# A 128-column expert visit in the common form, and two transposes of the next tokens moved into the arms

## The chip, the core and the metric

The kernel runs on one core of a Trainium2 chip, one launch. The metric is device time in microseconds; lower is better.

## What is computed

Attention with rotary embedding over 4 batches, 8 heads, 576 positions, 64 dimensions; then an RMS-normed gated layer on the 2304 tokens; then a layer of eight experts, of which each token takes one:

```python
logits = x @ w_gate + modality_bias[modality_id]
e_idx = np.argmax(logits, axis=1)
...
for e in range(E):
    mask = e_idx == e
    if not mask.any():
        continue
    h = np.maximum(x[mask] @ w1[e], 0.0)
    out[mask] = gate_w[mask, None] * (h @ w2[e])
```

Here x[mask] has 512 columns, w1[e] is 512 by 1024 and w2[e] is 1024 by 512. The change lies in this last loop alone.

## The kernel before

Every float32 product is made of three: an operand is split into a high part (rounded to the matmul's float32 format, on ACT) and a low part (what is left, by a subtraction on DVE), and high by high, low by high and high by low are summed.

The expert layer is a row of **visits** (moe, body). One visit serves up to 384 tokens of one expert; an expert with more tokens gets several. Which expert, and how many tokens, is known only on the chip, so each of the 14 possible visits is written out with five **arms**, one for each size in SIZES (128, 256, 288, 352, 384 tokens), and body's choose branches to one by a value that each engine loads. In the program the 128 arm stands right behind the comparisons; the arms of 384, 352, 288 and 256 follow it in this order, and then the tail, which all arms share. Each engine has its own copy of this program and its own branches. With these inputs visits 0 to 7 run; their sizes are 384, 288, 256, 256, 384, 352, 128 and 352 (visit 0 has no arms).

A common arm (visit) has eight steps of first-layer products: 12 matmuls per step (line 1339), the weights being the stationary operand and the N tokens the moving one, so that the hidden values come out transposed; a ReLU on ACT (line 1342) and a subtraction on DVE (line 1343) then give their high and low parts. Four more steps (two for 256 tokens) make the second-layer sums of the second and third block of 128 tokens: second issues 12 matmuls of 512 columns (line 1426) per step, and put scales the sums on DVE and scatters them by an indirect DMA from POOL. The second layer of the first 128 tokens is made in the tail, for every size.

The 128 arm (small_visit) is different: the tokens are the stationary operand, the weights the moving one, 24 matmuls of 512 columns (line 1378). The hidden values come out with tokens on partitions; after the ReLU (line 1383), eight transposes (turn, line 1368) bring them into the form that second needs.

Around these products each visit prepares the next one:

- gather fetches the next visit's tokens by three indirect DMAs from POOL; xT transposes a block of 128 tokens (4 matmuls against the identity, line 1323, into one of two PSUM banks that take turns, then a copy on ACT and a subtraction on DVE, lines 1325 and 1326). A third xT has to wait until the first one's bank has been read by DVE.
- wsplit splits the next pieces of weights (ACT line 1297, DVE line 1298) into a ring of 11; wload then issues the DMA of a later piece, 512 KB, into the raw buffer that the split has freed. So a load is issued when a split on DVE ends. The table SPLITS says after which step of an arm which pieces are split, by the number of 128-token blocks.

The order on each engine is the order in which this code is written.

Of the kernel before, what the change touches and what calls it, by code (L numbers as in the profile page):

```python
# [16 lines left out]
AF = mybir.ActivationFunctionType  # L17
ALU = mybir.AluOpType
# [5 lines left out]
P = 128  # L24
# [7 lines left out]
def fr(ap):  # L32
    return ap.bitcast(F32)
# [17 lines left out]
class Kernel:  # L51
# [824 lines left out]
NE, VT, NV = 8, 384, 14  # L876
# [4 lines left out]
SPLIT0 = {1: 7, 3: 8, 5: 9, 7: 10, 8: 11, 9: 12, 10: 13, 11: 14, 12: 15, 13: 16}  # L881
SPLITS = [
    {},
    {0: 9, 5: 11, 9: 13},
    {0: 8, 1: 9, 3: 10, 5: 11, 8: 12, 9: 13},
    {0: 8, 1: 9, 3: 10, 5: 11, 8: 12, 10: 13},
]
TURNS = {8: (0,), 9: (1,), 10: (2,)}
SIZES = (128, 256, 288, 352, 384)


# [19 lines left out]
class Fused(Kernel):  # L911
# [443 lines left out]
                yield s  # L1355
                s += 1

    def small_visit(self, v):

        nc, st = self.nc, self.st  # L1360
        xh, xl = self.xTt
        ix, xs = st.pop(("x", v))
        hs = [x[:, 0:512] for x in xs[1:3]]

        def turn(x):
            ps = self.p_h().rearrange("p (k n) -> p k n", k=4)
            for k in range(4):
                nc.tensor.transpose(ps[:, k], hs[x][:, k * P:(k + 1) * P], self.idf)
            h, l = (y[:, :, 0:P] for y in self.hq[x::2])
            nc.scalar.copy(h, ps)  # L1370
            nc.vector.tensor_tensor(l, ps, fr(h), op=ALU.subtract)

        for x in range(2):
            ps = self.p_o()
            for k in range(4):
                wh, wl = (y[:, x * 512:(x + 1) * 512] for y in self.wpc[8 * v + k])
                for i, (l, r) in enumerate(((xh, wh), (xl, wh), (xh, wl))):
                    nc.tensor.matmul(ps, l[:, k, 0:P], r, start=(k == 0 and i == 0), stop=(k == 3 and i == 2))
                if x == 1 and k == 1:
                    turn(0)  # L1380
                if k < 3:
                    yield 4 * x + k
            nc.scalar.activation(hs[x], ps, AF.Relu)
            if x == 1:
                g = self.gates(xs, 1)
            yield 4 * x + 3
        turn(1)
        st["last", v] = ix, g
        yield 8
        yield 9  # L1390

    def tail(self, v):

        ix, g = self.st.pop(("last", v))
        ps = self.p_o()
        more = v + 1 < NV
        if more:
            self.xT(v + 1, 0)
            self.wsplit(8 * v + 14)
            self.xT(v + 1, 1)  # L1400
        self.second(v, ps, 0, 0, P)
        if more:
            self.xT(v + 1, 2)
            self.wsplit(8 * v + 15)
        self.second(v, ps, 1, 0, P)
        self.put(ps, ix, g, 0, P)

    def hidden(self, f):
# [25 lines left out]
    def ahead(self, v, s, nt=3):  # L1434

        if v == 0 and s >= 8:
            for t in TURNS.get(s, ()):
                self.xT(1, t)
        i = SPLITS[nt] if v else SPLIT0
        if s in i:  # L1440
            self.wsplit(8 * v + i[s])
# [16 lines left out]
    def body(self, v):  # L1458

        s = self.state()  # L1460

        def arm(x):
            N = SIZES[x]
            if N == P and v + 1 < NV:
                self.gather(v + 1)
            for y in self.visit(v, N) if N > P else self.small_visit(v):
                if y == 0 and N > P and v + 1 < NV:
                    self.gather(v + 1)
                self.ahead(v, y, (N + P - 1) // P)

        def choose(x):
            if x == 0:
                arm(0)
                return
            with self.tc.If(self.size(v) > x - 1, preferred_fallthrough_block=False) as cmp:  # L1475
                arm(x)
            self.restore(s)
            with cmp.Else():
                choose(x - 1)

        choose(len(SIZES) - 1)
# [166 lines left out]
```

## Time and profile before

| | |
|---|---|
| device time, median of 3 runs | 1110.79 us (1108.62 to 1111.71) |
| the profiled execution's own time | 1116.74 us |
| its span, first to last instruction | 1115.0 us |
| TensorE busy | 1037.2 us, 93% of the span |
| DVE, ACT, POOL busy | 64%, 41%, 30% |
| mean granted clock of TensorE | 0.981 of full speed |
| expert visits 1 to 7 | from about 890 to 1103 us of the span |

The profile's view of time sums instructions by line; a timeline gives them in order, with the idle time of the engine ahead of an instruction and what ended it. "issue" there means that the engine waited for nothing that the profile shows.

### The profile page before, as it was taken

How to read it: one execution, taken by the hardware profiler on the slowest of the kernel's cores; microseconds unless marked ns; L12 is line 12 of the kernel's file. 1: busy time of each engine (PE TensorE's matmuls, PEld its weight loads, DVE VectorE, ACT ScalarE, POOL GpSimd, SP SyncE). 2: the span in 40 equal slices, each digit the busy share in tenths (PEclk: the TensorE clock that was granted, in tenths of full speed). 3: DMA queues.
4: the chain of work that ended last, by engine and by line, in shares of the span. 5: the costliest groups of instructions: out<-in, count | busy, mean ns of one | idle time of the engine just before them, and what ended most of it. 6: DMA issues, size and time to landing. Idle time of an engine off the chain costs nothing. (4 is left out here: it accounts for less than half of the span.)

```text
span 1115.0 us, 18245 instructions
## 1 busy us (share of the span) xinstructions
PE 1037.2 (93%) x6662; PEld 878.8 (79%) x6662; DVE 710.4 (64%) x1362; ACT 459.3 (41%) x959; POOL 331.1 (30%) x372
## 2 busy tenths in 40 slices
PE   4999999989998899999999999999998999998795
PEld 3767777666776689899999999998877787898594
DVE  7686788897765876456465555562457856655652
ACT  2655666555555443322222222222235444444441
POOL 7756567478421401012011111110010222222211
PEclk9899999999999899999999999999999999999988
DMA  5333454444231102111131111100146656655653
GB/s 134 81 99 95 107 134 108 121 121 107 60 103 36 55 29 60 54 38 48 36 129 48 39 38 48 39 20 29 58 157 187 218 179 203 204 179 165 213 182 106
DMA packets 75708, 113.35 MB, mean 102 GB/s; under 512 B 18520, under 2 KB 43376, under 8 KB 75570
## 3 DMA queue, kind: packets, MB, share of 16 engines
q1 hardware_dynamic: 71890, 99.72, 30.2%
q0 software_dynamic: 3680, 11.91, 2.9%
q8 instruction: 72, 1.18, 0.4%
q14 instruction: 66, 0.54, 0.1%
HBM read 85.39 MB, written 12.17 MB: 88 GB/s over the span
## 5 line engine op out<-in xcount | busy, mean ns | idle before, releaser
L771 PE MATMUL gv<-xh,whi 128*128 128x384 f32 x576 | 197.2, 342 | 1.4 <-ACT xh L749 1.4
L771 PE MATMUL gv<-xl,whi 128*128 128x384 f32 x576 | 195.2, 339 | 0.2 <-DVE xl L753 0.2
L771 PE MATMUL gv<-xh,wlo 128*128 128x384 f32 x576 | 194.7, 338 | 0.0
L288 DVE TENSOR_REDUCE m<-s 128x1 fp32r<-128x576 f32 (+1 forms) x160 | 119.9, 752 | 66.4 <-PE s L287 65.1
L670 POOL TENSOR_TENSOR wlo<-cvt,whi 128x256 fp32r<-128x256 f32 x66 | 50.8, 774 | 338.2 <-ACT whi L669 338.1
L781 DVE TENSOR_TENSOR s<-s,gv 128x384 f32<-128x384 f32 x72 | 39.8, 554 | 154.0 <-PE gv L771 145.1
L315 ACT ACTIVATE E<-sT 128x576 f32<-128x576 f32 (+1 forms) x160 | 104.3, 653 | 64.7 <-PE sT L314 60.9
L771 PEld LDWEIGHTS gv<-xh,whi 128*128 128x128 f32 x576 | 108.7, 189 | 6.6 <-issue 3.4
L780 ACT ACTIVATE s<-gv 128x384 f32<-128x384 f32 x72 | 34.9, 492 | 189.4 <-PE gv L771 189.4
L771 PEld LDWEIGHTS gv<-xl,whi 128*128 128x128 f32 x576 | 108.8, 189 | 1.9 <-DVE xl L753 0.4
L771 PEld LDWEIGHTS gv<-xh,wlo 128*128 128x128 f32 x576 | 108.6, 188 | 0.0
L312 PE MATMUL sT<-qkT 128*128 128x288 f32 (+1 forms) x320 | 80.6, 334 | 10.2 <-DVE m L288 6.1
L326 PE MATMUL av<-E,vraw 128*64 128x288 f32 x640 | 88.5, 421 | 1.6 <-ACT sq L337 1.6
L799 PE MATMUL yps<-whi,hh 128*128 128x512 f32 x216 | 87.2, 404 | 2.3 <-ACT yacc L804 1.3
L814 DVE TENSOR_TENSOR yacc<-yacc,yps 128x512 f32<-128x512 f32 x99 | 67.7, 686 | 32.2 <-PE yps L799 30.8
L287 PE MATMUL s<-qkT 128*128 128x288 f32 (+1 forms) x320 | 79.6, 335 | 6.6 <-ACT qkT L273 2.7
L799 PE MATMUL yps<-wlo,hh 128*128 128x512 f32 x216 | 85.3, 395 | 0.0
L799 PE MATMUL yps<-whi,hl 128*128 128x512 f32 x216 | 85.2, 394 | 0.0
L1313 POOL DMA_INDIRECT x<-ysc,ix x27 | 30.3, 1121 | 143.1 <-DVE e L1139 76.7
L314 PE MATMUL sT<-qB,kB 65*128 65x288 f32 (+1 forms) x320 | 70.8, 304 | 1.8 <-issue 1.5
L1432 POOL DMA_INDIRECT out<-cvt,ix x20 | 25.3, 1265 | 156.1 <-DVE cvt L1430 120.2
L326 PEld LDWEIGHTS av<-E,vraw 128*64 128x64 f32 x640 | 43.7, 140 | 34.4 <-issue 6.2
(287 smaller groups left out, 2048.8 us busy)
## 6 DMA issues: line engine op xcount, KB each, us to landing
raw<-in_w SPq DMA_DIRECT2D x52, 512.0 KB
stt<-in_w SPq DMA_DIRECT2D x25, 512.0 KB
stt<-in_w_gate SPq DMA_DIRECT2D x24, 256.0 KB
stt<-in_w_val SPq DMA_DIRECT2D x24, 256.0 KB
stt<-in_w_out SPq DMA_DIRECT2D x24, 256.0 KB
kB<-qkT SPq DMA_DIRECT2D x32, 144.0 KB
qB<-qkT SPq DMA_DIRECT2D x32, 144.0 KB
qkT<-qkT SPq DMA_DIRECT2D x32, 144.0 KB
```

The source lines that it names most:

```text
L287: nc.tensor.matmul(s[:n, u, 0:288], qA[:, j * 128:j * 128 + n], kA[:, u * 288:u * 288 + 288], start=True, stop=True)
L288: nc.vector.tensor_reduce(m[:n, j:j + 1], s[:n, :, 0:288], axis=AX.XY, op=ALU.max)
L312: nc.tensor.matmul(s[:n, u, 0:288], kA[:, j * 128:j * 128 + n], qA[:, u * 288:u * 288 + 288], start=True, stop=False)
L314: nc.tensor.matmul(s[:n, u, 0:288], kB[0:65, j * 128:j * 128 + n], qB[0:65, u * 288:u * 288 + 288], start=False, stop=True)
L315: nc.scalar.activation(e.rearrange("p (u c) -> p u c", u=2), s[:n, :, 0:288], AF.Exp, scale=0.125)
L326: self.nc.tensor.matmul(av[64 * h:64 * h + 64, 0:288], V[:, h, j * 64:j * 64 + 64], E[:, h if j < 4 else 0, j, 288 * u:288 * u + 288], sta ...
L670: nc.gpsimd.tensor_tensor(lo, f, fr(hi), op=ALU.subtract)
L771: nc.tensor.matmul(t[:, :CH], w[:, k], r[:, k], start=(n == 0), stop=(n == 11))
L780: nc.scalar.activation(s, ps[0][:, :CH], AF.Silu)
L781: nc.vector.tensor_tensor(s, s, ps[1][:, :CH], op=ALU.mult)
L799: nc.tensor.matmul(ps, l, r[:, 2], start=(n == 0), stop=(n == tot - 1))
L814: nc.vector.tensor_tensor(old[:, t], old[:, t], ps, op=ALU.add)
```

## The change

small_visit is removed: the 128 arm is visit(v, 128), eight steps of 12 matmuls with 128 moving columns. Two of the three xT of the next tokens, blocks 0 and 1, move from the tail into the arm, by the table TURNS: for 128 tokens both after step 7, for 256 after steps 8 and 9, for larger sizes after steps 10 and 11. The third, block 2, stands first in the tail, and the 24 second-layer matmuls follow it without another transpose between them. The splits of the 128 arm stand after steps 0, 5 and 7 (before: 0, 5 and 9). gather in the 128 arm stands after the first step.

```diff
--- before.py
+++ after.py
@@ -881,11 +881,11 @@
 SPLIT0 = {1: 7, 3: 8, 5: 9, 7: 10, 8: 11, 9: 12, 10: 13, 11: 14, 12: 15, 13: 16}
 SPLITS = [
     {},
-    {0: 9, 5: 11, 9: 13},
+    {0: 9, 5: 11, 7: 13},
     {0: 8, 1: 9, 3: 10, 5: 11, 8: 12, 9: 13},
     {0: 8, 1: 9, 3: 10, 5: 11, 8: 12, 10: 13},
 ]
-TURNS = {8: (0,), 9: (1,), 10: (2,)}
+TURNS = [{8: (0,), 9: (1,), 10: (2,)}, {7: (0, 1)}, {8: (0,), 9: (1,)}, {10: (0,), 11: (1,)}]
 SIZES = (128, 256, 288, 352, 384)
 
 
@@ -1355,54 +1355,17 @@
                 yield s
                 s += 1
 
-    def small_visit(self, v):
-
-        nc, st = self.nc, self.st
-        xh, xl = self.xTt
-        ix, xs = st.pop(("x", v))
-        hs = [x[:, 0:512] for x in xs[1:3]]
-
-        def turn(x):
-            ps = self.p_h().rearrange("p (k n) -> p k n", k=4)
-            for k in range(4):
-                nc.tensor.transpose(ps[:, k], hs[x][:, k * P:(k + 1) * P], self.idf)
-            h, l = (y[:, :, 0:P] for y in self.hq[x::2])
-            nc.scalar.copy(h, ps)
-            nc.vector.tensor_tensor(l, ps, fr(h), op=ALU.subtract)
-
+    def tail(self, v):
+
+        ix, g = self.st.pop(("last", v))
+        if v + 1 < NV:
+            self.xT(v + 1, 2)
+            self.wsplit(8 * v + 14)
+        ps = self.p_o()
         for x in range(2):
-            ps = self.p_o()
-            for k in range(4):
-                wh, wl = (y[:, x * 512:(x + 1) * 512] for y in self.wpc[8 * v + k])
-                for i, (l, r) in enumerate(((xh, wh), (xl, wh), (xh, wl))):
-                    nc.tensor.matmul(ps, l[:, k, 0:P], r, start=(k == 0 and i == 0), stop=(k == 3 and i == 2))
-                if x == 1 and k == 1:
-                    turn(0)
-                if k < 3:
-                    yield 4 * x + k
-            nc.scalar.activation(hs[x], ps, AF.Relu)
-            if x == 1:
-                g = self.gates(xs, 1)
-            yield 4 * x + 3
-        turn(1)
-        st["last", v] = ix, g
-        yield 8
-        yield 9
-
-    def tail(self, v):
-
-        ix, g = self.st.pop(("last", v))
-        ps = self.p_o()
-        more = v + 1 < NV
-        if more:
-            self.xT(v + 1, 0)
-            self.wsplit(8 * v + 14)
-            self.xT(v + 1, 1)
-        self.second(v, ps, 0, 0, P)
-        if more:
-            self.xT(v + 1, 2)
-            self.wsplit(8 * v + 15)
-        self.second(v, ps, 1, 0, P)
+            self.second(v, ps, x, 0, P)
+            if x == 0 and v + 1 < NV:
+                self.wsplit(8 * v + 15)
         self.put(ps, ix, g, 0, P)
 
     def hidden(self, f):
@@ -1434,7 +1397,7 @@
     def ahead(self, v, s, nt=3):
 
         if v == 0 and s >= 8:
-            for t in TURNS.get(s, ()):
+            for t in TURNS[0].get(s, ()):
                 self.xT(1, t)
         i = SPLITS[nt] if v else SPLIT0
         if s in i:
@@ -1461,12 +1424,14 @@
 
         def arm(x):
             N = SIZES[x]
-            if N == P and v + 1 < NV:
-                self.gather(v + 1)
-            for y in self.visit(v, N) if N > P else self.small_visit(v):
-                if y == 0 and N > P and v + 1 < NV:
+            nt = (N + P - 1) // P
+            for y in self.visit(v, N):
+                if y == 0 and v + 1 < NV:
                     self.gather(v + 1)
-                self.ahead(v, y, (N + P - 1) // P)
+                self.ahead(v, y, nt)
+                if v + 1 < NV:
+                    for t in TURNS[nt].get(y, ()):
+                        self.xT(v + 1, t)
 
         def choose(x):
             if x == 0:
```

On TensorE, the whole 128 arm of visit 1 stood like this (po, ph, pt and pc are PSUM banks, W and Wl weight pieces, idf the identity, hq and xT the transposed hidden values and tokens, x gathered tokens):

```order
L1378 MATMUL po_8761<-Wl_8743,xT 128x512 x3
L1378 MATMUL po_8761<-Wl_8744,xT 128x512 x3
L1378 MATMUL po_8761<-Wl_8745,xT 128x512 x3
L1378 MATMUL po_8761<-W_8426,xT 128x512 x3
L1378 MATMUL po_8759<-Wl_8743,xT 128x512 x3
L1378 MATMUL po_8759<-Wl_8744,xT 128x512 x3
L1368 MATMUL ph_8758<-idf,x_8751 128x128 x4
L1378 MATMUL po_8759<-Wl_8745,xT 128x512 x3
L1378 MATMUL po_8759<-W_8426,xT 128x512 x3
L1368 MATMUL ph_8756<-idf,x_8752 128x128 x4
L1475 UNCONDITIONAL_BRANCH
```

Now it ends like this, after seven steps of the same four rows:

```order
L1339 MATMUL ph_8756<-xT,Wl_8743 128x128 x3
L1339 MATMUL ph_8756<-xT,Wl_8744 128x128 x3
L1339 MATMUL ph_8756<-xT,Wl_8745 128x128 x3
L1339 MATMUL ph_8756<-xT,W_8426 128x128 x3
L1323 MATMUL pc_6112<-idf,x_8439 128x128 x4
L1323 MATMUL pt_6111<-idf,x_8440 128x128 x4
L1440 UNCONDITIONAL_BRANCH
```

The 24 products and 8 transposes of before are 96 products, and eight transposes of the next tokens stand ahead of the branch.

On TensorE, the end of the 384 arm and the tail of visit 1 stood like this:

```order
L1426 MATMUL po_8759<-W_8429,hq 128x512 x6
...
L1426 MATMUL po_8759<-W_8430,hq 128x512
L1475 UNCONDITIONAL_BRANCH
...
L1323 MATMUL pc_6112<-idf,x_8439 128x128 x4
L1323 MATMUL pt_6111<-idf,x_8440 128x128 x4
L1426 MATMUL po_8760<-W_8427,hq 128x512 x6
L1426 MATMUL po_8760<-W_8428,hq 128x512 x6
L1323 MATMUL pc_6112<-idf,x_8441 128x128 x4
...
L1426 MATMUL po_8760<-W_8430,hq 128x512
L1265 TENSOR_LOAD vi
L1475 COMPARE_AND_BRANCH x4
```

And now:

```order
L1389 MATMUL po_8759<-W_8428,hq 128x512 x6
L1323 MATMUL pc_6112<-idf,x_8439 128x128 x4
L1389 MATMUL po_8759<-W_8429,hq 128x512 x6
...
L1389 MATMUL po_8759<-W_8430,hq 128x512
L1323 MATMUL pt_6111<-idf,x_8440 128x128 x4
L1440 UNCONDITIONAL_BRANCH
...
L1323 MATMUL pc_6112<-idf,x_8441 128x128 x4
L1389 MATMUL po_8761<-W_8427,hq 128x512 x6
L1389 MATMUL po_8761<-W_8428,hq 128x512 x6
L1389 MATMUL po_8761<-W_8429,hq 128x512 x6
...
L1389 MATMUL po_8761<-W_8430,hq 128x512
L1265 TENSOR_LOAD vi
L1440 COMPARE_AND_BRANCH x4
```

The second step of the last block stands between two transposes, and the branch follows the second of them; the tail has one transpose and then 24 products in a row up to the next visit's TENSOR_LOAD and comparisons.

On DVE, the end of the 128 arm, from step 5 on, is now (g is the gate, raw and stt are raw weights):

```order
L1298 TENSOR_TENSOR Wl_8741<-stt,Wl_8741 128x1024
L1298 TENSOR_TENSOR Wl_8742<-raw_8422,Wl_8742 128x1024
L1343 SCALAR_TENSOR_TENSOR hq<-ph_8758,hq 128x128
L1343 SCALAR_TENSOR_TENSOR hq<-ph_8756,hq 128x128
L1298 TENSOR_TENSOR Wl_8743<-raw_8423,Wl_8743 128x1024
L1298 TENSOR_TENSOR Wl_8744<-raw_8424,Wl_8744 128x1024
L1326 TENSOR_TENSOR xT<-pc_6112,xT 128x4x128
L1326 TENSOR_TENSOR xT<-pt_6111,xT 128x4x128
L1440 UNCONDITIONAL_BRANCH
```

The two subtractions of xT stand behind four splits.

## Rows read from the trace of the kernel before

**Rows 1.** Timeline of TensorE, the visits: start us, us, engine, line, what, [idle <-released by].

```profile
923.29 11.64 PE L1339 MATMUL ph<-xT,Wl 128*128 128x256 f32 x96 [2.35 <-issue]
934.77 2.96 PE L1426 MATMUL po<-Wl,hq 128*128 128x512 f32 x12
...
949.69 1.31 PE L1339 MATMUL ph<-xT,W 128*128 128x256 f32 x9 [2.33 <-issue]
...
998.94 2.98 PE L1426 MATMUL po<-Wl,hq 128*128 128x512 f32 x12
1001.75 0.60 PE L1323 MATMUL pt<-idf,x 128*128 128x128 f32 x4
1002.19 0.60 PE L1323 MATMUL pc<-idf,x 128*128 128x128 f32 x4
...
1005.75 3.06 PE L1426 MATMUL po<-Wl,hq 128*128 128x512 f32 x12
1011.76 15.63 PE L1339 MATMUL ph<-xT,Wl 128*128 128x352 f32 x96 [2.95 <-issue]
...
1045.36 0.84 PE L1378 MATMUL po<-W,xT 128*128 128x512 f32 x3
...
1053.26 0.66 PE L1368 MATMUL ph<-idf,x 128*128 128x128 f32 x4 [1.71 <-ACT x L1383]
1059.77 1.08 PE L1323 MATMUL pt<-idf,x 128*128 128x128 f32 x4 [5.85 <-issue]
...
1061.36 4.63 PE L1426 MATMUL po<-Wl,hq 128*128 128x512 f32 x12
...
1069.05 15.63 PE L1339 MATMUL ph<-xT,W 128*128 128x352 f32 x96
```

**Rows 2.** Branches of line 1475 on TensorE's queue, five stretches: ns min/median/max.

```profile
L1475 PEldq COMPARE_BRANCH  x2: 64/2613/5162, 917.8 to 918.0; - x2
...
L1475 PEldq COMPARE_BRANCH  x1: 3553/3553/3553, 997.6 to 997.6; - x1
...
L1475 PEldq COMPARE_BRANCH  x1: 6189/6189/6189, 1005.5 to 1005.5; - x1
...
L1475 PEldq COMPARE_BRANCH  x1: 6333/6333/6333, 1053.3 to 1053.3; - x1
...
L1475 PEldq COMPARE_BRANCH  x1: 433/433/433, 1066.0 to 1066.0; - x1
```

**Rows 3.** DMA, 997.5 to 999.2 us: queue, packets, MB, share of the engines.

```profile
q8 instruction: 1, 0.02, 3.5%
```

**Rows 4.** DMA, 999.2 to 1003 us.

```profile
q1 hardware_dynamic: 144, 0.52, 53.8%
```

**Rows 5.** DMA, 1006 to 1009.3 us.

```profile
q1 hardware_dynamic: 143, 0.52, 64.5%
```

**Rows 6.** DMA, 1009.3 to 1010.4 us.

```profile
q8 instruction: 1, 0.02, 5.4%
```

**Rows 7.** Groups by line and form: busy us, mean ns | idle before.

```profile
L1426 PEld LDWEIGHTS po<-W,hq 128*128 128x128 f32 x180 | 33.2, 188 | 6.7
...
L1298 DVE TENSOR_TENSOR Wl<-raw,Wl 128x1024 fp32r<-128x1024 f32 x24 | 29.3, 1222 | 5.5 <-ACT Wl L1297 5.4
...
L1297 ACT CAST Wl<-raw 128x1024 fp32r<-128x1024 f32 x24 | 24.9, 1043 | 0.0
...
L1343 DVE SCALAR_TENSOR_TENSOR hq<-ph,hq 128x384 fp32r<-128x384 f32 x16 | 8.8, 552 | 6.2 <-ACT hq L1342 4.6 <-issue 1.6
...
L1326 DVE TENSOR_TENSOR xT<-pc,xT 128x512 fp32r<-128x512 f32 x11 | 7.6, 689 | 4.4 <-ACT xT L1325 4.4
...
L1343 DVE SCALAR_TENSOR_TENSOR hq<-ph,hq 128x256 fp32r<-128x256 f32 x16 | 6.6, 421 | 8.3 <-ACT hq L1342 8.3
...
L1426 PEld LDWEIGHTS po<-W,hq 128*32 128x32 f32 x24 | 2.6, 109 | 2.9
```

**Rows 8.** Window 1054 to 1060 us: busy us of each engine, granted clock, DMA.

```profile
1054.00:1060.00 6.00, 0.23 (x1) 0.26 (x2) 3.44 (x6) 2.47 (x3) 0.00 (x0) 0.55 0.99 353
```

More of the change, by code (lines that the diff above doesn't have):

```diff
@@ L1356, in visit @@
                 s += 1
-    def small_visit(self, v):
-        nc, st = self.nc, self.st
-        xh, xl = self.xTt
-        ix, xs = st.pop(("x", v))
-        hs = [x[:, 0:512] for x in xs[1:3]]
-        def turn(x):
-            ps = self.p_h().rearrange("p (k n) -> p k n", k=4)
-            for k in range(4):
-                nc.tensor.transpose(ps[:, k], hs[x][:, k * P:(k + 1) * P], self.idf)
-            h, l = (y[:, :, 0:P] for y in self.hq[x::2])
-            nc.scalar.copy(h, ps)
-            nc.vector.tensor_tensor(l, ps, fr(h), op=ALU.subtract)
-        for x in range(2):
-            ps = self.p_o()
-            for k in range(4):
-                wh, wl = (y[:, x * 512:(x + 1) * 512] for y in self.wpc[8 * v + k])
-                for i, (l, r) in enumerate(((xh, wh), (xl, wh), (xh, wl))):
-                    nc.tensor.matmul(ps, l[:, k, 0:P], r, start=(k == 0 and i == 0), stop=(k == 3 and i == 2))
-                if x == 1 and k == 1:
-                    turn(0)
-                if k < 3:
-                    yield 4 * x + k
-            nc.scalar.activation(hs[x], ps, AF.Relu)
-            if x == 1:
-                g = self.gates(xs, 1)
-            yield 4 * x + 3
-        turn(1)
-        st["last", v] = ix, g
-        yield 8
-        yield 9
     def tail(self, v):
         ix, g = self.st.pop(("last", v))
+        if v + 1 < NV:
+            self.xT(v + 1, 2)
+            self.wsplit(8 * v + 14)
         ps = self.p_o()
-        more = v + 1 < NV
-        if more:
-            self.xT(v + 1, 0)
-            self.wsplit(8 * v + 14)
-            self.xT(v + 1, 1)
-        self.second(v, ps, 0, 0, P)
-        if more:
-            self.xT(v + 1, 2)
-            self.wsplit(8 * v + 15)
-        self.second(v, ps, 1, 0, P)
+        for x in range(2):
+            self.second(v, ps, x, 0, P)
+            if x == 0 and v + 1 < NV:
+                self.wsplit(8 * v + 15)
         self.put(ps, ix, g, 0, P)
```

## The prediction, made before the changed kernel ran

> **What bounds the kernel now.** I read four views: the timeline of TensorE over the expert visits, TensorE's branches, the DMA queues around two of them, and the groups by form. In the timeline TensorE works without a break inside a visit; the gaps the change can touch stand at the ends of arms and tails, and nearly all say "issue": ahead of visit 2 (2.35 us), visit 3 (2.33) and visit 5 (2.95), and 1.71 and 5.85 in the 128 arm, which is visit 6 [rows 1]. That visit takes 1069.05 - 1045.36 = 23.7 us up to the next one's first product.
>
> The gaps are branches. TensorE's queue runs ahead of the engine: the branch that ends visit 4's arm began at 997.6 [rows 2], while the arm's last matmul ended about 1001.75, 4.15 us later. Twelve 512-column matmuls take 1001.75 - 998.94 = 2.81 us, 0.234 each [rows 1], so some 17.7 matmuls were queued. A far jump has to bring a page of instructions (one packet of 0.02 MB [rows 3]): that branch took 3.55 us, the one into visit 5's arm 6.19, the one out of the 128 arm 6.33 [rows 2]. The page comes by DMA and waits behind a weight load that is already moving. For visit 4's arm it moved before 999.2 and the load after that [rows 3, 4]: short. For visit 5's entry the load moved first, and the page only after 1009.3 [rows 5, 6]; the branch ended at 1011.7, 2.3 us after the load: long. So a branch costs what its duration exceeds the work queued behind it, and its duration depends on whether it or a load comes first.
>
> The last gap has a second price. Between 1054 and 1060 the granted clock was 0.55 [rows 8], that is mostly the lower level (1.2 GHz), after TensorE had done 0.23 us of work. The work from 1059.77 to 1069.05, 9.3 us, is three transposes of blocks (0.44 each, by 1002.19 - 1001.75) and 24 matmuls (5.6), 6.9 us at full clock [rows 1]: 2.4 us lost.
>
> **The change, part by part.**
>
> *Entries of visits 2, 3 and 5.* Before, the last 17.7 queued matmuls of a tail were 12 products and 5.7 transposes (0.11 each): 3.4 us. Now all are products: 4.15, less some 0.8 us for the value's load and the comparisons. More important, the load. Before, the tail's first split freed a raw buffer about when the branch came: branch at 1005.5, load moving from 1006 on [rows 2, 5]. Now that split stands behind the third xT: on DVE it follows put and two xT of 0.69, and takes 1.22 [rows 7], while the branch comes 0.7 earlier, so I put the load's issue about 1 us after the branch. The page then goes first, a fetch is 3.55 us, and 0.2 us stays exposed. Visit 2 gains 2.35 - 0.2 = 2.15, visit 5 gains 2.95 - 0.2 = 2.75. Visit 3 follows a 256 arm, which splits once more after its last step; that load is still in front of the page, and I give this entry 1.0. Sum: -5.9. Bounds: -0.7 each by cover alone (-2.1), and all three gaps gone (-7.6).
>
> *Ends of the arms of visits 4, 5 and 7.* Now the last 17.7 are 4 transposes, 12 products and 1.7 transposes: 0.44 + 2.81 + 0.2 = 3.45 us, and the branch comes at 1002.6 - 3.45 = 999.1 in visit 4's times (the arm's work ends 0.88 later, by two xT). The load there is issued by a split behind the put of the second block, which the change doesn't move; it was moving from 999.2 on [rows 4], and a page comes about a microsecond after its branch. So the page that was ahead of the load is now behind it: to 1003 [rows 4], and 2.3 us more as at visit 5's entry: 1005.3. TensorE is done at 1002.6, a gap of 2.7. For visits 5 and 7 I take 2.0 each, their loads being no later but perhaps shorter. Sum: +6.7. Bounds: 3.55 against 3.45 of cover, 0.1 each (+0.3); 3.0 each (+9.0). Visit 1 (288) jumps only over the 256 arm, and the 256 arms fall into the tail: no far jump, nothing.
>
> *Visit 6, the 128 arm.* Removed: 24 products and 8 transposes with a wait for ACT between (1.71). Added: 96 products of 128 columns, each with its own weight load. No row shows such a pair. From above: 256 columns take (934.77 - 923.29)/96 = 0.120. From below: 0.234 at 512 and 0.120 at 256 give 0.00045 per column, so 0.062 at 128 if columns alone counted. Weight loads take 188 ns for 128 columns and 109 for 32 [rows 7], 0.82 ns per column, 105 ns for 128; between the bounds I take the load, with the few ns between pairs 0.112: 10.8 us, and 0.88 for two xT. A page of the Trainium skill ("TensorE: Matmul & The Clock Gate", section on the back-to-back issue gap) gives some 81 ns per pair at 128 columns in a sustained stream; by that the products would take 7.8 us and visit 6 end about 2.3 earlier. No run here shows it.
>
> What follows decides more. The tail's xT of block 2 needs the PSUM bank of block 0, and block 0's DVE subtraction stands behind four splits. Step 5 ends at 6 x 12 x 0.112 = 8.1; ACT's ReLU, gate and first split (1.04) take it to about 10.1; then DVE has four splits of 1.22, two hidden subtractions (552 at 384 and 421 at 256 columns give 0.29 at 128) and one xT of 0.69 [rows 7]: 6.2, so 16.3. TensorE has finished at 11.7: a gap of 4.6 in place of 1.71 and 5.85. The arm's branch (9.7 to at most 16) is hidden in it. Then 0.44 + 24 x 0.234 = 6.1: 22.4. A gap of this size I expect to cost the clock again, 2.4: 24.8 against 23.7, +1.1. Bounds: -3.5 (pairs of 81 ns or less, and no fall) to +3.
>
> *Visit 7's entry.* The same jump took 6.19 in visit 5 and 0.433 here [rows 2]. It passes the 128 and the 384 arm: 32 + 144 matmuls before, 104 + 152 now, each with a weight load, so some 350 and 510 instructions. I count it as far now: 3.55 us against 3.4 of cover, 0.1 (bounds 0 and 2.8, the long fetch). The Trainium skill ("Runtime: NRT & Kernel Launch", instruction fetch mechanics) says instructions come in blocks of 256, two at a time, and that a taken branch outside the two stalls for a fetch. By it this jump is always far and the longer arms speak against the change; the two durations here agree with it. The sum is the same by both, since the cover is counted from rows.
>
> Splits, ReLUs, gather and scatters keep their number; they lie beside TensorE's work outside visit 6, and if that cover went, the next late thing would be the first xT of the next visit.
>
> **Sum:** -5.9 + 6.7 + 1.1 + 0.1 = +2.0 us. The profiled execution's own time, 1116.74 (span 1115.0 and 1.7 around it), would become 1118.7. The median of the runs is 1110.79, six below it; I carry the difference over: **1112.8**.
>
> **Rivals.**
>
> *The arm-end branches stay ahead of the loads.* The race is lost by under a microsecond (999.1 plus about 1, against 999.2); a longer queue wins it. Then +0.3 instead of +6.7: -4.4, 1106.4. For it: the pages came first in the rows of before [rows 3, 4]. Against: one transposed block moved ahead of the branch is already 0.44.
>
> *Pages wait at both ends (slower).* The tail's load comes before the entry's branch as it did at visit 5 [rows 5, 6]; the entries then keep only the better cover, -2.1, beside +6.7 and +1.1: +5.8, 1116.6. It decides if the tail's split ends more than about 1 us earlier than I worked out.
>
> *Half clock after the new gaps.* The clock fell in the gap of 5.85 [rows 8], and no such loss stands behind that of 2.95: visit 5's 96 matmuls of 352 columns took 15.63 us, as visit 7's did [rows 1]. If gaps of 2 to 2.7 suffice, three times 2.4 more: +9.2, 1120.0.
>
> That the change doesn't do what it says: the 128 arm runs once with these inputs, at 1045.36 [rows 1], so it acts, but in one visit only.
>
> **Numbers.** A measurement here tells about 0.3%, 3.3 us, from no change. Forecast 0.48, first rival 0.25, second 0.18, third 0.09. The forecast's own range, 1109.5 to 1115.5, leaves a little on the slower side. Faster by over 0.3%: the first rival, nearly all, 0.22; slower: the other two and a little, 0.29; the same 0.49. The range goes from the first rival's centre, 1106, to a little over the second's, 1118.5.
>
> **What would show it.** Gaps ahead of visits 2 and 5 under 1 us and ahead of 3 about 1.3; new gaps of about 2 to 2.7 between the second transposed block of an arm and the third in visits 4, 5 and 7; in visit 6 products of 0.112 each and a gap of about 4.6 ahead of the tail's transposes, ended by DVE's xT, with a fall of the clock. A pair price over 0.12 in the 128 arm, gaps at all entries as before, or no gaps at the arms' ends, would prove it wrong.

## The result, and the profile after

The changed kernel takes 1126.82 us (median of 6 runs, 1123.03 to 1130.47), the kernel before in the same runs 1111.76 (1108.62 to 1114.94): the ratio is 1.0132, 95% interval 1.0103 to 1.0161. It is slower by 15 us. The forecast was 1112.8, the range ended at 1118.5.

The profiled execution after took 1128.17 us (span 1126.3, mean granted clock 0.979). The profiled execution of before stood 5 us over its median, this one 1.4, so I don't compare the spans but the visits. From visit 1's first product to visit 7's, 178.96 us before (890.09 to 1069.05) became 190.44 (887.61 to 1078.05): 11.5 us more. Visit 7 itself, from its first product to the last, took 33.7 us and takes 37.9.

The timeline of TensorE after, in the columns of [rows 1]; line 1389 is what line 1426 was (second-layer products), 1323 a transposed block, 1339 a first-layer product:

```profile
887.61 2.53 PE L1339 MATMUL ph<-xT,Wl 128*128 128x288 f32 x9 [1.98 <-issue]
...
914.41 0.66 PE L1323 MATMUL pc<-idf,x 128*128 128x128 f32 x4 [0.40 <-DVE cvt L1393]
914.83 5.71 PE L1389 MATMUL po<-W,hq 128*128 128x512 f32 x24
921.09 11.63 PE L1339 MATMUL ph<-xT,Wl 128*128 128x256 f32 x96 [0.55 <-issue]
...
940.69 0.66 PE L1323 MATMUL pt<-idf,x 128*128 128x128 f32 x4 [1.54 <-DVE Wl L1298]
...
947.65 1.30 PE L1339 MATMUL ph<-xT,W 128*128 128x256 f32 x9 [0.74 <-issue]
...
951.13 0.39 PE L1339 MATMUL ph<-xT,W 128*128 128x256 f32 x1 [0.87 <-issue]
...
968.47 0.66 PE L1323 MATMUL pc<-idf,x 128*128 128x128 f32 x4 [1.54 <-DVE W L1298]
...
1006.21 0.63 PE L1323 MATMUL pt<-idf,x 128*128 128x128 f32 x4 [2.57 <-issue]
1006.59 4.59 PE L1389 MATMUL po<-W,hq 128*128 128x512 f32 x12
...
1013.81 15.53 PE L1339 MATMUL ph<-xT,Wl 128*128 128x352 f32 x96
...
1044.03 0.63 PE L1323 MATMUL pc<-idf,x 128*128 128x128 f32 x4 [2.79 <-issue]
1044.41 7.33 PE L1389 MATMUL po<-W,hq 128*128 128x512 f32 x24
1051.58 0.44 PE L1339 MATMUL ph<-xT,W 128*128 128x128 f32 x3
...
1063.54 0.66 PE L1323 MATMUL pc<-idf,x 128*128 128x128 f32 x4 [0.26 <-DMA x<-ysc,ix]
1068.62 1.08 PE L1323 MATMUL pt<-idf,x 128*128 128x128 f32 x4 [4.42 <-DVE xT L1326]
...
1074.78 1.56 PE L1389 MATMUL po<-W,hq 128*128 128x512 f32 x6
1078.05 4.11 PE L1339 MATMUL ph<-xT,W 128*128 128x352 f32 x24 [1.72 <-issue]
...
1108.15 0.63 PE L1323 MATMUL pc<-idf,x 128*128 128x128 f32 x4 [2.41 <-issue]
1108.53 7.40 PE L1389 MATMUL po<-Wl,hq 128*128 128x512 f32 x24
```

Read against [rows 1]:

- The entries of visits 2, 3 and 5 waited 2.35, 2.33 and 2.95 us and now wait 0.55, 0.74 and 0 (the row of 1013.81 has no bracket): -6.3.
- New gaps stand between the second and the third transposed block of visits 4, 5 and 7: 2.57 + 2.79 + 2.41 = +7.8.
- Behind each of them 24 second-layer products take 7.2 to 7.4 us where, at 914.83, 24 take 5.71: +1.5, +1.6 and +1.7, in all +4.8.
- New waits ended by DVE stand ahead of the third block where the arm doesn't jump (visits 1, 2 and 3): 0.40 + 1.54 + 1.54 = +3.5.
- In visit 3's arm a stall of 0.87 is new, and visit 7's entry waits 1.72 where it waited not at all: +2.6.
- Visit 6 up to that wait takes 1078.05 - 1.72 - 1051.58 = 24.75 against 23.69: +1.1.
- The half clock in visit 1's arm: 9 products of 2.53 us where before they took 1.47 (row below): +1.1 in these alone.

That is 14.6 in sum, of the 15.7 by which visits 1 to 7 differ in these two profiles and of the 15 between the medians. The same nine products in the timeline of the kernel before:

```profile
890.09 1.47 PE L1339 MATMUL ph<-xT,Wl 128*128 128x288 f32 x9 [0.86 <-issue]
```

The branches that end the arms of visits 4, 5, 6 and 7, and the one into visit 7's arm, as rows of line 1440 on TensorE's queue, ns as min/median/max (before: 3553 for visit 4's, 433 for visit 7's entry [rows 2]):

```profile
L1440 PEldq COMPARE_BRANCH  x1: 5985/5985/5985, 1000.1 to 1000.1; - x1
...
L1440 PEldq COMPARE_BRANCH  x1: 5768/5768/5768, 1037.7 to 1037.7; - x1
...
L1440 PEldq COMPARE_BRANCH  x1: 4900/4900/4900, 1063.5 to 1063.5; - x1
...
L1440 PEldq COMPARE_BRANCH  x1: 5807/5807/5807, 1102.2 to 1102.2; - x1
...
L1440 PEldq COMPARE_BRANCH  x2: 67/2181/4295, 1073.6 to 1073.7; - x2
```

DMA after in 1000 to 1003.1 us, and then in 1003.1 to 1004.7: first the weight load (q1), then the page of instructions (q8). Before, the page came first [rows 3, 4]:

```profile
q1 hardware_dynamic: 144, 0.52, 78.9%
...
q8 instruction: 1, 0.02, 3.7%
```

And the granted clock in visit 1's arm, behind the new gaps and behind visit 6's (window; busy us of PE, PEld, DVE, ACT, POOL; clock; DMA share; GB/s), half of full, that is 1.2 GHz; before, only visit 6 had such a stretch [rows 8]:

```profile
887.60:891.00 3.40, 3.39 (x14) 3.39 (x15) 0.00 (x0) 0.11 (x1) 0.80 (x1) 0.50 0.76 177
...
1007.00:1010.40 3.40, 3.40 (x10) 2.61 (x9) 2.61 (x3) 2.39 (x3) 0.00 (x0) 0.50 0.17 63
1044.60:1048.00 3.40, 3.40 (x10) 2.66 (x9) 2.39 (x3) 2.48 (x3) 0.00 (x0) 0.50 0.02 4
1068.50:1071.90 3.40, 3.28 (x10) 2.83 (x11) 1.25 (x2) 2.12 (x3) 0.00 (x0) 0.50 0.59 202
1109.50:1112.80 3.30, 3.30 (x9) 2.55 (x9) 3.03 (x3) 1.83 (x2) 0.00 (x0) 0.50 0.06 19
```

### The profile page after: what moved, and what is told of

It is laid out like the page before. It is cut to its first block, busy times and chain, and to the rows that moved or that the text cites. A ratio compares the mean times of both kernels' runs of the same rounds, so it can differ in the third digit from the quotient of the medians.

```text
span 1126.3 us, 18410 instructions
## 1 busy us (share of the span) xinstructions
PE 1047.0 (93%) x6726; PEld 890.2 (79%) x6726; DVE 709.9 (63%) x1368; ACT 459.7 (41%) x963; POOL 331.7 (29%) x372
## 5 line engine op out<-in xcount | busy, mean ns | idle before, releaser
L326 PE MATMUL av<-E,vraw 128*64 128x288 f32 x640 | 86.2, 413 | 0.2 <-ACT sq L337 0.2
L1339 PE MATMUL ph<-xT,W 128*128 128x384 f32 (+4 forms) x384 | 66.6, 319 | 4.3 <-issue 3.3
```

The costliest lines, as they stand in the source:

```text
L326: self.nc.tensor.matmul(av[64 * h:64 * h + 64, 0:288], V[:, h, j * 64:j * 64 + 64], E[:, h if j < 4 else 0, j, 288 * u:288 * u + 288], sta ...
L1339: nc.tensor.matmul(ps[:, :N], w, x[:, k, 0:N], start=(i == 0), stop=(i == 11))
```

## The experiments

Two theories were to be told apart. Theory 1: the moved transposes cost the time, in two ways; (a) the arm-end branch comes later than a weight load, so its page waits, a gap opens and the clock falls behind it; (b) the third block needs the PSUM bank of the first, which DVE has not yet read. Theory 2: the 128-column form costs it, with 96 weight loads in place of 24 and longer code to jump over. Ratios are to the kernel before, run on the same chip in the same rounds, with 95% intervals; the expectations in microseconds were written beside its 1111.8, while on the two chips of these runs it took 1114 to 1115, so the ratios decide.

### The new 128 arm alone

The kernel before, with `visit(v, 128)` in place of `small_visit` and its tail unchanged:

```diff
-    {0: 9, 5: 11, 9: 13},
+    {0: 9, 5: 11, 7: 13},
...
-            for y in self.visit(v, N) if N > P else self.small_visit(v):
-                if y == 0 and N > P and v + 1 < NV:
+            for y in self.visit(v, N):
+                if y == 0 and v + 1 < NV:
```

> The new 128 arm alone: it runs the common form (96 products of 128 columns), the three transposes of the next tokens stay in the tail. Theory 1 (the moved transposes are the cost): arms and tails of the other visits keep the queue of before, so no gaps of 2.4 to 2.8 us at the arm ends of visits 4, 5 and 7, no half clock behind them, entries of visits 2, 3 and 5 wait 2 to 3 us as before; visit 6 takes 22 to 26 us; median 1109 to 1115 beside 1111.8 of the kernel before. Theory 2 (the 128-column form is the cost, with 96 weight loads in place of 24 and the longer jump): most of the 15 us is there already, 1121 to 1128.

Measured: 1.0012 (0.9998 to 1.0027), 1.3 us, which can't be told from nothing. Visit 6 took 24.2 us up to visit 7's first product (1051.83 to 1076.05), 23.7 before, with 1.49 at visit 7's entry. Theory 2 falls as the main cause. The profiled execution also showed something that the kernel before had not. Its timeline at visits 2 and 7, and the granted clock behind the entries of visits 2, 3 and 5:

```profile
925.39 13.04 PE L1339 MATMUL ph<-xT,Wl 128*128 128x256 f32 x96 [1.97 <-issue]
...
1076.05 15.63 PE L1339 MATMUL ph<-xT,W 128*128 128x352 f32 x96 [1.49 <-issue]
```

```profile
925.40:930.00 4.60, 4.60 (x26) 4.60 (x27) 1.17 (x4) 1.32 (x2) 0.99 (x1) 0.63 0.45 162
953.40:957.00 3.60, 3.60 (x18) 3.60 (x19) 0.24 (x1) 0.73 (x2) 0.00 (x0) 0.53 0.51 181
1016.90:1022.00 5.10, 5.10 (x23) 5.10 (x24) 1.58 (x4) 1.40 (x2) 0.98 (x1) 0.67 0.24 91
```

Behind gaps of 1.97, 2.16 and 2.57 us the clock fell; behind the same three gaps before, which were longer, it did not (11.64 us for visit 2's 96 products [rows 1], 13.04 here). This execution took 1123.24 us, the longest of the twelve, whose median is 1115.98; so three half clocks at once need not be this kernel's usual case.

### The moved transposes alone

The changed kernel, with `small_visit` and its splits back for 128 tokens; its other arms and the tail stay as they are:

```diff
-    {0: 9, 5: 11, 7: 13},
+    {0: 9, 5: 11, 9: 13},
...
-TURNS = [{8: (0,), 9: (1,), 10: (2,)}, {7: (0, 1)}, {8: (0,), 9: (1,)}, {10: (0,), 11: (1,)}]
+TURNS = [{8: (0,), 9: (1,), 10: (2,)}, {8: (0,), 9: (1,)}, {8: (0,), 9: (1,)}, {10: (0,), 11: (1,)}]
...
-            for y in self.visit(v, N):
+            for y in self.visit(v, N) if N > P else self.small_visit(v):
```

> The moved transposes alone: two transposed blocks of the next tokens stand in every arm and one first in the tail, but the 128 arm keeps its own form with 512 columns. Theory 1: gaps of 2.4 to 2.8 us at the arm ends of visits 4, 5 and 7, each with some 3.4 us of half clock behind it, waits of about 1.5 us for a PSUM bank ahead of the third transposed block after the 256 arms; median 1120 to 1127. Theory 2: only the entries' gain remains, 1104 to 1111. Either way visit 7's entry tells whether the longer 128 arm is what makes that jump far: 4 us of branch as in the changed kernel, or 0.4 as before, worth about 1.7 us.

Measured: 1.0092 (1.0070 to 1.0113), 10 us. The timeline has the gaps of theory 1 at the same places, with the half clock behind them (12 products in 4.59 us), here visit 4's arm end:

```profile
1000.08 0.63 PE L1323 MATMUL pt<-idf,x 128*128 128x128 f32 x4 [2.62 <-issue]
1000.46 4.59 PE L1423 MATMUL po<-W,hq 128*128 128x512 f32 x12
```

Two parts of the expectation failed. The waits ahead of the third block were 0 after the 288 arm and 0.41 after the 256 arms, not 0.40 and 1.54, though these arms are the changed kernel's own; what that means is said under the third block's bank below. And visit 7's branch took 4.72 us though the 128 arm had its old form: with eight more transposes in each arm that jump is far, and with the new form alone it is far too (4.61). Its length alone doesn't decide: the same jump over 176 matmuls was far at visit 5's entry of the kernel before (6.19) and near at visit 7's (0.43) [rows 2]. What put it within reach there was not looked into.

The two parts alone give 10 and 1.3 us, together 11.6 of 15. What they cost only together is mostly these waits (0.40 + 1.13 + 1.13 more in the changed kernel) and visit 7's entry (1.72 against 0.52).

### The load behind the arm-end branch

The changed kernel, with an arm's last split one step later; the split sets off the weight load:

```diff
-    {0: 8, 1: 9, 3: 10, 5: 11, 8: 12, 10: 13},
+    {0: 8, 1: 9, 3: 10, 5: 11, 8: 12, 11: 13},
```

> The changed kernel, with the last split of the arms of 288 to 384 tokens one step later, after step 11 in place of step 10: the weight load that it sets off comes later than the arm-end branch. Theory 1a (the page of instructions waits behind the weight load): the branches at the arm ends of visits 4, 5 and 7 go from 5.8 us to 3.4 to 4, their gaps from 2.4 to 2.8 us to under 0.6, and the half clock behind them goes: 7 to 12 us less than the changed kernel, 1115 to 1120. Rival (the branch is long by itself, because of the queue it stands in): branches stay at 5.8 us, median 1125 to 1129. A third outcome, the load only moves on to the next jump: arm-end gaps gone but entries of visits 5 and 6 wait 2 us more, 1119 to 1124.

Measured: 1.0065 (1.0045 to 1.0084); against 1.0132 that is 7.4 us less. The branches of visits 4, 5 and 7 took 3.91, 3.59 and 3.34 us, the page came at once, with no row of q1 in the window (DMA, 1002.4 to 1005 us, the row of q8), and no half clock stood in visits 1 to 5 or 7. Branch, DMA and timeline at visit 4's arm end:

```profile
L1440 PEldq COMPARE_BRANCH  x1: 3913/3913/3913, 1002.4 to 1002.4; - x1
```

```profile
q8 instruction: 1, 0.02, 2.3%
```

```profile
1007.54 0.66 PE L1323 MATMUL pt<-idf,x 128*128 128x128 f32 x4 [1.54 <-DVE W L1298]
```

Theory 1a is shown: one step of a split, with no instruction added or taken away, makes the branch 2.1 us shorter. In the gap's place stands a wait of 1.54 for the bank. The moved split makes most of it: visit 1's arm, which has no far branch at its end, now waits 1.53 there where it waited 0.40 (the next experiment shows how). So an arm end gives back about 1.0 of its gap and 1.6 of clock, three times 2.6, beside the 7.4 measured; smaller changes elsewhere, this one and visit 7's entry (0.76 in place of 1.72) among them, nearly cancel.

### The third block in a bank of its own

```diff
-            self.xT(v + 1, 2)
+            self.xT(v + 1, 2, self.p_h)
```

> The changed kernel, with the third transposed block written to a PSUM bank of the other ring, so that it need not wait for DVE to read the first block. Theory 1b (the waits of 1.54, 1.54 and 0.40 us ended by DVE ahead of the third block are that bank): these three waits go, 3 us or more; in visit 6 the wait of 4.42 us ends at the branch at the earliest (1063.55 + 4.90 = 1068.45 against 1068.62), so it stays but says issue; median 1122 to 1124. Rival (the wait is DVE's for another reason, or the branches end no earlier): 1126 to 1128.

Measured: 1.0105 (1.0084 to 1.0125), 3.0 us less than the changed kernel; the intervals overlap, so the time alone shows little, and the timeline decides. The three waits went (at visit 1's end the third block follows the second at once), and one gap grew: visit 3's entry, 0.74 in the changed kernel, behind a branch of 5.62 us:

```profile
910.90 0.60 PE L1323 MATMUL ph<-idf,x 128*128 128x128 f32 x4
...
943.72 1.30 PE L1339 MATMUL ph<-xT,W 128*128 128x256 f32 x9 [2.26 <-issue]
```

In visit 6 the wait stayed, 4.58, and the row now says issue: it is the branch's.

So the shared bank causes the three waits, but not in the way of theory 1b: DVE was not late in reading it. In the changed kernel the subtraction that reads visit 2's first block (in bank pt) was over at 937.34. TensorE's third block, in the same bank, began at 940.69, just behind a split that stands later on DVE:

```profile
936.65 0.69 DVE L1326 TENSOR_TENSOR xT<-pt,xT 128x512 fp32r<-128x512 f32 x1 [1.25 <-ACT xT L1325]
...
939.42 1.22 DVE L1298 TENSOR_TENSOR Wl<-stt,Wl 128x1024 fp32r<-128x1024 f32 x1
```

The tail is one program for all five arms. In the changed kernel each of the three waits ended with the last but one DVE instruction of the arm (put's scaling after the 288 arm, a split after the 256 arms), and in the 128 arm the last but one is the subtraction of block 0. With the old 128 arm, where two splits stand between the two subtractions, the waits ended with the last but two or were gone. So it looks as if the tail waits for one count of DVE's instructions that is safe after every arm, and the 128 arm, though visits 1 to 3 don't run it, sets the count. For this speaks that the edits of the second experiment lie in the 128 arm alone and shortened the waits of visits 1, 2 and 3, and that the split moved later, which became the last but one after the larger arms, lengthened visit 1's. No run moved block 0 in the 128 arm by itself.

### Both

```diff
-    {0: 8, 1: 9, 3: 10, 5: 11, 8: 12, 10: 13},
+    {0: 8, 1: 9, 3: 10, 5: 11, 8: 12, 11: 13},
...
-            self.xT(v + 1, 2)
+            self.xT(v + 1, 2, self.p_h)
```

> The changed kernel with both edits: the arm's last split after step 11, the third transposed block in a PSUM bank of the other ring. Theory 1: with the split moved six waits of 1.53 us for the bank were left (visits 1 to 5 and 7), so 6 x 1.53 = 9.2 us go on top of the 7.4 that the split's place gave: 16.6 of the changed kernel's 15 us excess, that is no more than 2 to 3 us from the kernel before on either side, ratio 0.997 to 1.002. Rival (behind each bank wait stands a branch that the wait only hides, so one gap takes the other's place): the two edits do not add up, 5 to 8 us over the kernel before, ratio 1.004 to 1.007.

Measured: 1.0034 (1.0014 to 1.0053), just outside what theory 1 expected and short of the rival, with an interval that reaches into both. The six waits of 1.53 went (0.34, 0.76 and 0.39 were left at the three arm ends), but only 3.5 us came off (1.0065 to 1.0034), not 9.2. The timeline and the branch at visit 5's entry say why:

```profile
1007.86 17.19 PE L1339 MATMUL ph<-xT,Wl 128*128 128x352 f32 x96 [1.80 <-issue]
```

```profile
L1440 PEldq COMPARE_BRANCH  x1: 5469/5469/5469, 1002.3 to 1002.3; - x1
```

The load that the late split sets off is now under way when the tail's branch comes, since the tail begins 1.5 us earlier; that page waits in its place (loads from 1001.99 on, the page at 1005.42), and the clock fell once more (17.19 us where 15.63 stood [rows 1]). Visit 3's entry waited 2.07.

### Both, with the old 128 arm

The same with `small_visit`, as in the second experiment:

```diff
-            for y in self.visit(v, N):
+            for y in self.visit(v, N) if N > P else self.small_visit(v):
```

> Both edits, and the 128 arm in its own form with 512 columns. Theory 1 with the 128-column form at no profit: visit 6 is 1.5 to 2 us shorter than with both edits and the new form (24.7 against 26.5 us in the runs so far), 3 to 0 us under the kernel before, ratio 0.996 to 1.000. Rival (visit 6 costs the same by either form once the bank is free): as with the new form, within 1 us of it.

Measured: 1.0053 (1.0033 to 1.0072), which neither expected. Visit 6 was 1.1 us shorter than with the new form (25.1 against 26.2), but in this profile the clock fell there for 10.2 us, and visit 7's second half lost 1.8 more. The two intervals overlap: what the old form is worth in this arrangement stays open.

### The load ahead of both branches

The changed kernel, its third block in the other bank, and the last two splits of an arm earlier, ahead of the scaling of the second block on DVE:

```diff
-    {0: 8, 1: 9, 3: 10, 5: 11, 8: 12, 9: 13},
-    {0: 8, 1: 9, 3: 10, 5: 11, 8: 12, 10: 13},
+    {0: 8, 1: 9, 3: 10, 5: 11, 7: 12, 8: 13},
+    {0: 8, 1: 9, 3: 10, 5: 11, 7: 12, 8: 13},
...
-            self.xT(v + 1, 2)
+            self.xT(v + 1, 2, self.p_h)
```

> The changed kernel with the third block in the other bank, and the last two splits of an arm one to two steps earlier (after steps 7 and 8, ahead of the scaling of the second block) instead of later. Theory 1: the last load of the arm is then over before the arm-end branch begins, and the next one, set off in the tail, is issued after the entry's branch, so no jump meets a moving load: branches of 3.3 to 4.2 us at the arm ends of visits 4, 5 and 7 and at the entries of visits 2, 3 and 5, gaps there under 0.8 us. With both edits before (split later) 1.80 and 2.07 us stood at two entries and 3.4 us of half clock behind one; so 3 to 5 us less than that, ratio 0.997 to 1.001 to the kernel before. Rival (the jumps are long whenever two visits' loads are near): ratio 1.002 to 1.005 as with the split later.

Measured: 0.9993 (0.9970 to 1.0017), 15 us under the changed kernel. Branches at visit 4's arm end and visit 5's entry, then the timeline at that entry (0.24 at the arm end):

```profile
L1440 PEldq COMPARE_BRANCH  x1: 3657/3657/3657, 993.4 to 993.4; - x1
...
L1440 PEldq COMPARE_BRANCH  x1: 3687/3687/3687, 999.9 to 999.9; - x1
```

```profile
1003.69 1.55 PE L1339 MATMUL ph<-xT,Wl 128*128 128x352 f32 x8 [0.23 <-issue]
```

At the six jumps that the expectation names the branches took 3.33 to 3.69 us, and with the bank free as well the whole excess is gone. What keeps this version from a gain is visit 6 with visit 7's entry, 27.9 us (1037.66 to 1065.51) against 23.7: its gap ahead of the third block was 4.56, behind a branch of 5.04, and visit 7's entry waited 1.34 behind one of 5.63. And in visit 3's arm TensorE stood for 1.62 a few products after its entry, as it did for 0.87 in the changed kernel.

### The tail's order alone

The kernel before with its arms unchanged; in the tail the three blocks first, the third in the other bank:

```diff
             self.xT(v + 1, 0)
-            self.wsplit(8 * v + 14)
             self.xT(v + 1, 1)
+            self.xT(v + 1, 2, self.p_h)
+            self.wsplit(8 * v + 14)
         self.second(v, ps, 0, 0, P)
         if more:
-            self.xT(v + 1, 2)
             self.wsplit(8 * v + 15)
```

> The kernel before, with its arms as they are; only its tail is reordered: the three transposed blocks first, the third in a bank of the other ring, then the two splits and the 24 second-layer products without a transpose between. Theory 1: the arm ends keep their queue (no gaps there, no half clock), and the entries of visits 2, 3 and 5 get the longer queue and the page ahead of the load: gaps of 2.35, 2.33 and 2.95 us become 0.3 to 1.2 each, 4 to 6 us less than the kernel before, ratio 0.994 to 0.997; visit 6 keeps its gap of about 5.85. Rival (three transposes in a row wait for ACT and DVE as they did in the changed kernel, or the load still goes first): entries as before, ratio 0.999 to 1.003.

Measured: 0.9927 (0.9902 to 0.9953), 8 us faster than the kernel before, a little more than theory 1 expected. The timeline of the three entries and of visit 6:

```profile
922.47 11.63 PE L1339 MATMUL ph<-xT,Wl 128*128 128x256 f32 x96 [0.64 <-issue]
...
948.05 1.31 PE L1339 MATMUL ph<-xT,W 128*128 128x256 f32 x9 [1.53 <-issue]
...
1007.54 15.63 PE L1339 MATMUL ph<-xT,Wl 128*128 128x352 f32 x96 [0.39 <-issue]
...
1054.02 1.12 PE L1323 MATMUL pc<-idf,x 128*128 128x128 f32 x4 [4.66 <-issue]
```

The entries give 7.63 - 2.56 = 5.1 us, visit 6's gap 1.2 (5.85 before). So most of what the change had to give at the entries (6.3) comes from the tail's order; the transposes need not leave the tail for it, and left there they don't take the cover from the arm-end branch. Two things moved in that order: no transpose stands among the 24 products, and the splits, which set off the loads, stand behind the third block. The branches into visits 2, 3 and 5 became shorter, 3.83, 4.89 and 4.10 us for 5.16, 5.17 and 6.19; that is 3.7 of the 5.1, so the smaller part is cover. That the loads' place shortened them agrees with the experiments above; no run here separates the two.

### That tail with the new 128 arm, and with earlier splits

To the last kernel the edit of the first experiment is added:

> The reordered tail with the new 128 arm. By the runs so far the form alone cost 1.3 us (ratio 1.0012, 0.9998 to 1.0027), of which 1.49 us was visit 7's entry, where the branch became far; the reordered tail should hide most of that. Theory 1: within 1 us of the reordered tail with the old 128 arm, 3 to 6 us under the kernel before, ratio 0.994 to 0.998. Rival (three transposes in front of a visit 6 with short cover wait longer): 2 us or more above it.

Measured: 0.9927 (0.9901 to 0.9953), the same; visit 7's far jump (3.74 us) is hidden, as expected. Then, in the arms of 256 tokens, the last two splits earlier:

```diff
-    {0: 8, 1: 9, 3: 10, 5: 11, 8: 12, 9: 13},
+    {0: 8, 1: 9, 3: 10, 5: 11, 7: 12, 8: 13},
```

> The reordered tail with the new 128 arm, and in the arms of 256 tokens the last two splits after steps 7 and 8 in place of 8 and 9. Theory 1: the entry of visit 3, which waited 1.58 us behind a branch of 4.87 us, meets no moving load any more: 0.3 to 0.7 us; all else as in the kernel with the reordered tail and the new arm, so 1 us less than it, ratio 0.990 to 0.995 to the kernel before. Rival (that branch is long for another reason): 1.4 to 1.7 us as it was.

Measured: 0.9911 (0.9881 to 0.9942). Visit 3's entry and its branch:

```profile
943.67 1.30 PE L1339 MATMUL ph<-xT,W 128*128 128x256 f32 x9 [0.38 <-issue]
```

```profile
L1439 PEldq COMPARE_BRANCH  x1: 3487/3487/3487, 940.0 to 940.0; - x1
```

The entry went as expected, 1.58 to 0.38, but visit 7's entry waited 1.03 in place of 0.22 in this profile; the 1 us in time is within the intervals. These three are faster than both kernels.

## Why the prediction was wrong

**Entries of visits 2, 3 and 5: right.** Forecast -5.9, measured -6.3. Visits 2 and 5 keep 0.55 and 0, where 0.2 each was worked out; visit 3 gained 1.6 where 1.0 was given.

**Arm ends of visits 4, 5 and 7: right as far as the gap goes.** Forecast 2.7 + 2.0 + 2.0, measured 2.57 + 2.79 + 2.41 (7.8 for 6.7), with the load ahead of the page and a branch of 5.99 us, from 1000.05, where 6.2 was worked out. The split moved alone shows the cause.

**Visit 6: the time right, by luck in part.** It took 24.75 us for a forecast of 24.8. The products came at 1.34 us per 12 (the first 12 at 1.29), that is 0.112 each, as worked out. The Trainium skill ("TensorE: Matmul & The Clock Gate", back-to-back issue gap) has 81 ns per pair at 128 columns; the trace does not agree for these float32 products, and the measurement decides. The gap was 4.42 for 4.6, but it came another way. DVE's subtraction of block 0 ended at 1066.62 + 0.68 = 1067.30, 15.7 us after the visit's start where 16.3 was worked out, and alone would have made a gap of 3.1 (row: 1063.54 + 0.66 = 1064.20). What ended last was the arm's branch, which the prediction had as hidden: it began at 1063.55, with the second block, which had waited for its gathered tokens ([0.26 <-DMA]), took 4.90 and ended at 1068.45. The row of 1068.62 names DVE's xT, but with a bank of its own the third block waited 4.58, for "issue". The clock fell as expected, at 1.6 us rather than 2.4.

**The step that failed most: the half clock.** It was kept out of the sum and given a chance of 0.09, on the ground that no such loss stood behind visit 5's gap of 2.95. It came behind all three new gaps, at 1.5 to 1.7 us each (4.8), and once in visit 1's arm (1.1); the rival had 2.4 each. The evidence was one place in one execution. The new 128 arm alone shows how weak that was: the same three entries, with shorter gaps, had a half clock behind each of them. In the twelve traces 19 gaps of 1.8 to 3.2 us stand at the entries and arm ends of visits 2 to 5 and 7, and 13 have a half clock behind them. So in these kernels such a gap has to be priced with its clock as a likely case, not as a remote one. The 4.8 is read from one execution; but over the six runs of each kernel the mean granted clock was 0.978 and 0.977 where the three arm-end gaps stood (moved transposes alone, third block's own bank) and 0.984 in the same rounds with the split moved, where they didn't. The changed kernel's own six runs, taken earlier, had 0.981.

**The second: "the 256 arms fall into the tail: no far jump, nothing".** There is no jump, but the third block still shares the first one's bank. The text looked for that wait in visit 6 alone and put it at nothing in visits 1, 2 and 3, where it was 0.40, 1.54 and 1.54. To ask when DVE reads the bank, as the description of xT does, would not have found it: in visit 2 DVE had read it 3.3 us before the wait ended. Moving the block to another bank took the three waits away.

**The third: visit 7's entry,** 0.1 forecast, 1.72 measured. That the jump becomes far was right; the Trainium skill's rule on jumps outside the fetched blocks ("Runtime: NRT & Kernel Launch", instruction fetch mechanics) agrees with 0.43 turning into 4.30 us. The cover was mis-sized: from the branch at 1073.70 to the end of the last product, 1074.78 + 1.56 = 1076.34, it is 2.64 us and not 3.4, and the branch took 4.30 and not 3.55, since loads were moving from 1073.57 on and its page came at 1075.60.

The account in sum: between 1112.8 and 1126.8 lie 14.0 us. The half clock behind the arm ends has 4.8, the bank 3.5, visit 7's entry 1.6, the larger gaps 1.1, the clock in visit 1's arm 1.1, visit 3's stall 0.9, and the kernel before was itself 1.0 higher in these runs; the entries gave 0.4 more than forecast. That makes 13.6.

Of the rivals, the third happened, at two thirds of its price (4.8 for 7.2), beside the forecast's own terms. The first rival's condition, a branch ahead of the load, is what the split moved later brought about: it gave 7.4 us back. With the load moved ahead of the branch instead, and the bank free, the change is worth nothing in place of 15 us lost.

Visit 1's entry belongs to none of this. It waited 0.86 before and 1.98 after, but 0.93 to 1.87 in the ten other kernels, in no relation to their edits; its half clock appeared in two of the twelve traces.

## What to carry to other kernels

- A far branch costs what its fetch exceeds the work queued behind it, and the fetch is short or long by whether a large transfer is ahead of it: at the arm ends of visits 4, 5 and 7 it took 3.3 to 3.9 us without one and 5.8 to 6.2 behind one, in all twelve traces. When work is moved past a branch, look up which transfer is issued in the two microseconds around it, and move the transfer's trigger rather than the work.
- A gap of 2 to 3 us on TensorE may bring a half clock that costs 1.5 to 1.7 us more; price both.
- A block that is moved ahead of others in a ring of two buffers brings its reuse wait with it; check the wait at every place where the order now stands, not only at the one where it is longest. Where several arms lead to one tail, look in the trace at which instruction ends the wait: here it was not the one that read the buffer.

## What the runs showed that was not expected

Equal gaps had unequal results: 2.35, 2.33 and 2.95 us in the kernel before with the clock full behind them, 1.97, 2.16 and 2.57 in the kernel with the new 128 arm alone with 1.2 GHz behind each (granted clock 0.63, 0.53 and 0.67 of the windows shown). In other runs gaps of 2.07, 2.15 and 2.26 at visit 3's entry had the full clock behind them, and one of 1.80 at visit 5's had half. The length of the gap therefore doesn't decide it alone; what does was not tried. The Trainium skill ("TensorE: Matmul & The Clock Gate", the clock gate) says that the chip watches activity in stretches that run free of the program, by which the same gap could fall either way; no run here shows it.

Repairs did not add up: the split moved later closed the gaps at three arm ends and made bank waits of 1.53 there and in visit 1, and taking the six waits away gave 3.5 us in place of 9.2, in the main because two entries' branches then came behind loads. Only with the loads moved ahead as well was the whole excess gone.
